# A written-out order of 840 tasks, laid anew: attention with a decaying state and a SiLU layer on one core

## The chip, the core and the metric

The kernel runs on one core of one Trainium2 chip. A core has five engines that run side by side, each through its own list of instructions in order: PE (TensorE, matmuls and transposes; PEld is its loading of weights), ACT (ScalarE), DVE (VectorE), POOL (GpSimd) and SP (SyncE, which here only starts transfers). They wait for one another through semaphores, and DMA engines move data between HBM and the core's memory. The metric is the time of one execution in microseconds on the device. The span is the time from the first to the last instruction in the profiled execution.

## The reference

A recurrent attention over 768 steps, for 4 batches and 8 heads of 48 features, gives `x` of 3072 x 384, and a layer of width 2048 follows:

```python
f = 1.0 / (1.0 + np.exp(-f_logit))
for t in range(S):                      # S = 768, B = 4, H = 8, D = 48
    state = f[:, :, t, :, None] * state + np.einsum('bhd,bhe->bhde', k[:, :, t], v[:, :, t])
    y[:, :, t] = np.einsum('bhd,bhde->bhe', q[:, :, t], state)
x = y.transpose(0, 2, 1, 3).reshape(B * S, H * D)
h = x @ w_in                            # 384 x 2048
g = h * (1.0 / (1.0 + np.exp(-h)))
out = g @ w_out                         # 2048 x 384
```

Inputs and outputs are of float32; the kernel's matmuls are of bf16.

## The kernel before

**Tiles.** The 768 steps are cut into 6 chunks of 128. A chunk of a batch is a unit, of which there are 24, and two units make a pair; `PAIRS` lists 12. Pairs 0 to 3 (kind `T`) hold the first two chunks of one batch. Pairs 4 to 11 (kind `N`) hold the same chunk of two batches. In a chunk the running product of `f` is a sum of logarithms, done by a matmul with a triangular matrix; the queries are divided and the keys multiplied by its exponential, so that the recurrence becomes a masked product of 128 x 128, and a state of 48 x 48 for each head passes from chunk to chunk.

**Tasks.** The work of a pair `P` and, where it has one, of a unit `i` is cut into tasks. A word such as `qkD.9.0:S:1` of the string `PLAN` names task, pair and unit, then the engine (P = PE, A = ACT, V = DVE, G = POOL, S = SP) and the numbers of the buffers that it takes anew. The tasks are:

- `f`, `q`, `k`, `v`: loads (L227), of a pair or, where a word has two of them, of half a pair. `E`, `L`: exp (L233) and ln (L237, L240) on ACT. `cs`: the cumulative sum on PE (L304 to L314). `a`, `ia`: its exponentials on ACT (L316). `al`: the decay over a chunk, on ACT (L255, L318).
- `qg`, `ki`: queries and keys times those (L321). `vb`: `v` as bf16. `tq` and `qkc`: in pairs 0 to 3, PE transposes of `qk` (L328) and their copy. `qkD`: in pairs 4 to 11, a DMA transpose of `qk` in their place (L336).
- `sc`: scores on PE (L345, L349). `at`: the mask, on DVE (L353). `y` and `yi`: the output of attention on PE (L262, L361, L365). `d`, `sd`, `su`: the new state, on PE (L274, L382), DVE or ACT (L386, L181) and POOL (L392, two instructions each).
- `yc`: `y` as bf16. `yT` and `xc`: PE transposes of it (L373) and their copy, for pairs 0 to 5 and 9 and unit 1 of pair 6; `yD`: a DMA transpose in their place (L377).
- `mi.P.j` (L248): two of the 16 column blocks of `x @ w_in` for both units, six matmuls of 128 x 256. `si.P.j` (L253): their SiLU on ACT. `mo.P.i.n` (L285): four of the 16 matmuls of `g @ w_out` for one unit. `oc` and `so`: the copy of the result and its store (L296, where pairs 0 to 3 take two DMAs, and L298).
- `wi`, `wo`: loads of the weights, issued by POOL. `idle.W.n`: n matmuls of W columns on zeros (L435), with no result.

**What sets the order.** Nothing is planned at run time or by the compiler: the last loop of the kernel goes through the words of `PLAN` and emits them, so each engine has its tasks in the order in which they stand there. The first four loads are emitted ahead of all else. An engine waits where a task needs what another has not done yet, or a buffer that is still read. The number of buffers of each class is in `SLOTS` (for instance six for `q`, four for `hT`, eight PSUM banks `pb`), and which of them a task takes stands in its word. SP issues loads, stores and DMA transposes in one list, so a wait there holds all that is behind it.

**ACT's tables.** Exp and ln need one table of functions on ACT, SiLU another. Where two tasks that follow each other on ACT in the plan need different ones, a load of the table (L484) is emitted ahead of the second:

```python
modes = [(n, mode_of(kind)) for n, (kind, *_) in enumerate(plan) if mode_of(kind)]
turns = {n2: TABLES[m2] for (_, m), (n2, m2) in zip(modes, modes[1:]) if m != m2}
```

Copies on ACT need neither, and stand where they stand.

Of the kernel before, what the change touches and what calls it, by code (L numbers as in the profile page):

```python
# [43 lines left out]
al.1:A:5 qg.0.0:G:2 ki.0.1:V:3 idle.512.1::2 idle.256.1::2 cs.2.1:P:0 ia.2.1:A:2 sd.1.0:A:1 qg.0.1:V: y.1:P:1,2 ki.0.0:G: tq.0.0:P:6 q.2.0:S:4
su.1.0:G:0 tq.0.1:P:7 wi.0:G: a.2.1:A:1 al.2:A:1 yc.1.0:V:2 cs.2.0:P:5 yT.1.0:P:1 qkc.0.1:V:1 qkc.0.0:A: yi.1.1:P: sc.0.0:P:0,7 xc.1.0:V:0 yc.1.1:A:0
al.0:A:2 vb.0.1:A:3 at.0.0.0:V:0 yT.1.1:P:6 sc.0.1:P:2,1 vb.0.0:G:4 at.0.0.1:V: d.0:P:0,4 wi.2:G: xc.1.1:A: sd.0.0:A:0 at.0.1.1:V:1 at.0.1.0:V:
ia.2.0:A:3 su.0.0:G:0 mi.1.2:P:6 wo.0:G: mi.1.3:P:0 wo.1:G: y.0:P:1,2 yi.0.1:P: a.2.0:A:4 sd.1.1:V:1 k.2.0:S:4 mi.1.6:P:3 yc.0.0:A:0 yT.0.0:P:5
# [12 lines left out]
L.4.0:A:1 mo.2.1.3:P: mo.2.0.1:P: at.3.1.1:V: oc.2.1:A:0 qkD.5.0:S:3 E.6.0:A:0 L.6.0:A:2 vb.5.0:A:5 at.3.0.1:V: qkD.5.1:S:2 sd.3.1:V:1 sc.5.0:P:3,0  # L60
at.5.0.1:V:0 at.5.0.0:V: y.3:P:2,4 v.5.1:S: vb.5.1:G:6 sc.5.1:P:5,6 at.5.1.1:V:1 yi.3.1:P: cs.4.1:P:7 a.4.1:A:0 so.0.1:S: k.4.1:S:5 at.5.1.0:V:
mo.2.0.2:P: k.6.0:S:2 q.6.0:S:0 yc.3.0:A:1 yc.3.1:A:0 al.4.1:A:5 mo.2.0.3:P: oc.2.0:A:4 ia.4.1:A:2 y.5.0:P:6 cs.6.0:P:3 a.6.0:A:3 yc.5.0:V:2 q.4.1:S:4
yT.3.0:P:4 yT.3.1:P:0 xc.3.1:V:1 su.3.1:G:0 xc.3.0:V: cs.6.1:P:1 q.4.0:S: f.7.0:S:2 ki.4.1:V:1 ia.6.1:A:4 y.5.1:P:2 yc.5.1:V:1 yT.5.0:P:0 cs.4.0:P:6
# [453 lines left out]
```

## Time and profile before

| what | value |
|---|---|
| median of 3 runs | 176.43 us (175.55 to 177.61) |
| the profiled execution | 176.43 us |
| its span | 174.7 us, 4734 instructions |
| mean granted clock of PE | 0.998 |
| PE busy | 168.0 us (96%) |
| ACT busy | 128.8 us (74%) |
| DVE busy | 77.9 us (45%) |
| POOL busy | 64.6 us (37%) |
| moved by DMA | 32.12 MB, mean 184 GB/s |

In rows of groups there stand the line, the engine, the operation, what it writes and reads, and the count; then the busy time, the mean of one in ns, and the idle time ahead of it with what ended most of it. In rows of a timeline there stand the start, the duration, the engine, the line and the operation; in brackets the idle time before and what ended it. In the chain of waits SPq is the time that SP's queue took to issue.

### The profile page before, as it was taken

What the parts mean: (1) busy time and instruction counts of PE and PEld (TensorE: products, weight loads), DVE (VectorE), ACT (ScalarE), POOL (GpSimd) and SP (SyncE); (2) the same over time, 40 slices, a digit from 0 to 9 for tenths busy, and PEclk for the clock granted to TensorE, in tenths of its full rate; (3) what the DMA queues carried; (4) which work ended last, traced back from release to release, by engine and by line L of the source; (5) the groups of instructions that cost most, each with busy time, mean ns of one, the idle gap of its engine ahead of it and who ended that gap; (6) DMA issues with size and microseconds to landing.
All of it is one profiled execution on the core that took longest, in us unless ns stands there. A gap on an engine that the chain in (4) does not pass through costs nothing.

```text
span 174.7 us, 4734 instructions
## 1 busy us (share of the span) xinstructions
PE 168.0 (96%) x1921; PEld 125.1 (72%) x1921; DVE 77.9 (45%) x163; ACT 128.8 (74%) x236; POOL 64.6 (37%) x110
## 2 busy tenths in 40 slices
PE   7989999999999999999999999999998999999992
PEld 2547888666876897866786696776785866877870
DVE  7388700527749933245672421435912674410010
ACT  3799697384999999968888899887778741273811
POOL 6087891032484350224627004940053376100000
PEclk9999999999999999999999999999999999999999
DMA  5999999989958989899998895998995999221321
GB/s 142 324 325 218 267 201 203 280 204 234 220 110 184 203 171 207 191 199 181 195 228 178 159 231 132 241 189 170 193 186 153 208 145 238 82 45 40 140 94 45
DMA packets 110677, 32.12 MB, mean 184 GB/s; under 512 B 104096, under 2 KB 110528, under 8 KB 110656
## 3 DMA queue, kind: packets, MB, share of 16 engines
...
q10 hardware_dynamic: 672, 0.33, 0.6%
...
q14 instruction: 6, 0.05, 0.1%
HBM read 25.17 MB, written 4.72 MB: 171 GB/s over the span
## 4 chain that ended last, share of the span: by engine, by line
PE 77%; DMA 10%; SPq 5%; POOL 3%; ACT 2%; issue 1%; POOLq 0%
PE pb L248 33%; PE pb L285 31%; SPq L227 4%; DMA f<-in_f_logit_dram 4%; DMA k<-in_k_dram 3%; PE pb L349 2%; PE pb L361 2%; DMA qkT<-qk 2%; POOL qk L321 2%; PE pb L365 2%; PE pb L373 1%; DMA xT<-yb 1%; PE pb L311 1%; PE pb L328 1%; PE pb L382 1%
## 5 line engine op out<-in xcount | busy, mean ns | idle before, releaser
L285 PE MATMUL pb<-w_out_sb,hT 128*128 128x384 bf16 (+2 forms) x400 | 70.2, 320 | 0.0
L248 PE MATMUL pb<-xT,w_in_sb 128*128 128x256 bf16 x576 | 68.7, 273 | 0.6 <-DMA xT<-yb 0.6
L253 ACT ACTIVATE hT<-pb 128x512 bf16<-128x512 f32 x96 | 51.2, 612 | 22.3 <-PE pb L248 21.7
L248 PEld LDWEIGHTS <-w_in_sb 128*128 128x128 bf16 x576 | 55.1, 98 | 9.4 <-issue 0.8
L285 PEld LDWEIGHTS <-hT 128*128 128x128 bf16 x400 | 36.4, 98 | 19.1
L392 POOL TENSOR_TENSOR st<-sd,al 48x192 bf16<-48x192 f32 x40 | 20.5, 512 | 23.1 <-PE pb L361 8.8
L316 ACT ACTIVATE x<-pb 128x384 f32<-128x384 f32 x48 | 21.2, 505 | 5.1 <-PE pb L308 2.5
L353 DVE TENSOR_TENSOR atm<-pb,triu 128x512 bf16<-128x512 f32 x32 | 20.0, 683 | 9.7 <-PE pb L349 9.5
L321 POOL TENSOR_TENSOR qk<-k,x 128x384 bf16<-128x384 f32 x15 | 15.4, 1037 | 21.9 <-DMA k<-in_k_dram 11.7
L484 ACT ACT_TABLE_LOAD x17 | 21.8, 1283 | 0.3
L183 DVE COPY ob<-pb 128x384 f32<-128x384 f32 (+1 forms) x14 | 7.5, 534 | 22.9 <-ACT hT L253 13.4
L183 POOL CAST vb<-v 128x384 bf16<-128x384 f32 x16 | 8.9, 560 | 20.4 <-DMA v<-in_v_dram 20.1
L321 POOL TENSOR_TENSOR qk<-q,x 128x384 bf16<-128x384 f32 x9 | 9.2, 1031 | 18.2 <-ACT hT L253 11.6
L386 DVE TENSOR_TENSOR sd<-pb,st 128x384 f32<-128x384 f32 x16 | 8.8, 552 | 15.3 <-PE pb L382 7.1
L321 DVE TENSOR_TENSOR qk<-q,x 128x384 bf16<-128x384 f32 x15 | 9.3, 622 | 9.1 <-ACT x L316 4.2
L233 ACT ACTIVATE e<-f 128x768 f32<-128x768 f32 x12 | 10.1, 843 | 3.8 <-DMA f<-in_f_logit_dram 3.7
L353 DVE TENSOR_TENSOR atm<-pb,mask 128x512 bf16<-128x512 f32 x16 | 10.0, 683 | 3.2 <-PE pb L345 2.9
L183 DVE CAST yb<-pb 128x384 bf16<-128x384 f32 x13 | 7.1, 553 | 9.1 <-PE pb L365 4.1
L183 DVE COPY qkTT<-pb 128x1024 bf16<-128x1024 bf16 x6 | 4.1, 690 | 11.0 <-PE pb L328 10.9
L181 ACT COPY ob<-pb 128x384 f32<-128x384 f32 (+1 forms) x11 | 5.1, 470 | 5.2 <-PE pb L285 5.1
L435 PE MATMUL pb<-zero 128*128 128x512 bf16 (+1 forms) x20 | 7.1, 507 | 1.2 <-DVE halves L467 1.2
L181 ACT CAST yb<-pb 128x384 bf16<-128x384 f32 x11 | 5.2, 481 | 3.1 <-PE pb L365 2.2
...
## 6 DMA issues: line engine op xcount, KB each, us to landing
...
```

Source lines behind the costliest of these rows:

```text
L181: nc.scalar.copy(dst, src)
L183: ENG[eng].tensor_copy(dst, src)
L233: return nc.scalar.activation(e, at("f", P)[:, j * w:(j + 1) * w], AF.Exp, scale=-1.0)
L248: nc.tensor.matmul(h[:, i, cols], w_in_sb[:, kk, n * 128:(n + 1) * 128], at("xT", P)[:, kk, cols], start=(kk == 0), stop=(kk == KT - 1))
L253: return nc.scalar.activation(at("hT", P)[:, 2 * j:2 * j + 2, :], at("h", P, j).rearrange("p (n c) -> p n c", n=2), AF.Silu)
L285: nc.tensor.matmul(at("o" + key, P, i)[:, 0:cols.stop - cols.start], at("hT", P)[:, n, i * C:(i + 1) * C], w_out_sb[:, n, cols], start=(n ...
L316: nc.scalar.activation(at(kind, P, i).rearrange("p h d -> p (h d)"), at("cs", P, i)[:, 0:HD], AF.Exp, scale=1.0 if kind == "ia" else -1.0)
L321: ENG[eng].tensor_mul(at("qk", P, i)[:, j, :, 0:D], heads("qk"[j], P, i), at("ia" if j else "a", P, i))
L353: ENG[eng].tensor_mul(at("atm", P, i)[:, r], at(f"s{r}", P, i).rearrange("p (n c) -> p n c", c=C), mask[:, None, :].to_broadcast([C, NP, C]))
L386: nc.vector.tensor_add(at("sd", P, i), d_ps, prev_state(P, i))
L392: nc.gpsimd.tensor_mul(at("st", P, i)[lo:lo + D, :, r * D:(r + 1) * D], at("sd", P, i)[lo:lo + D, :, r * D:(r + 1) * D], al_of(P, i)[lo:lo ...
L484: nc.scalar.preload_act_table_set(turns[n])
```

## The change

The string `PLAN` is written anew. Code, pairs, buffers and their numbers are as before. The set of tasks is the same too, but for the idle matmuls: 17 of 512 columns become 18, and 3 of 256 become 4, in other places. Some 60 tasks change their engine: eight `vb` go from POOL to ACT and five from DVE to POOL, seven `ki` from POOL to DVE, six `qg` from DVE to POOL, six `yc` from ACT to DVE and four back, five `oc` from ACT to DVE. Loads of ACT's table become 19, from 17. Of the rows of the string, one of each side stands here for all; a line of the new kernel has a number that is higher by one, since the string has a row more.

```diff
@@ -37,70 +37,71 @@
 PLAN = """
...
-mo.7.0.0:P:7 sc.9.1:P:6,1 sc.9.0:P:4,5 at.9.1.0:V:1 at.9.0.0:V:3 si.7.5:A: mi.7.6:P:3 si.7.7:A: si.7.3:A: mo.7.0.1:P: at.9.0.1:V: at.9.1.1:V:
...
+mo.7.0.0:P:3 yT.9.0:P:5 sc.8.0:P:2,4 xc.9.1:V:3 ia.10.1:A:2 sc.8.1:P:0,6 L.11.0:A:1 mo.7.1.2:P: xc.9.0:V: su.9.1:G:0 mi.9.1:P:5 mi.9.4:P:1 si.9.4:A:2
...
 """
```

ACT, where the last SiLUs of pair 7 and those of pair 9 are, before: `si.7.6`, `yc.9.0`, a table load, `ia.10.1`, `a.10.1`, `E.11.0`, `L.11.0`, a table load, `si.9.2`, `si.9.6`. (`hT` is written by a `si`, `x` by an `ia` or `a`, `e` by an `E`, `lf` by an `L`.)

```order
L253 ACTIVATE hT_123<-pb_143 128x512
L181 CAST yb_117<-pb_144 128x384
L484 ACT_TABLE_LOAD
L316 ACTIVATE x_91<-pb_145 128x384
L316 ACTIVATE x_90<-pb_145 128x384
L233 ACTIVATE e_83<-f_63 128x768
L240 ACTIVATE lf_86<-e_83 128x16x48
L484 ACT_TABLE_LOAD
L253 ACTIVATE hT_122<-pb_145 128x512
L253 ACTIVATE hT_122<-pb_143 128x512
```

The same place in the new plan: `si.7.7`, a table load, `a.10.1`, `E.11.0`, `ia.10.1`, `L.11.0`, a table load, `si.9.4`, a table load, `a.11.0`, a table load, `si.9.3`.

```order
L254 ACTIVATE hT_122<-pb_144 128x512
L485 ACT_TABLE_LOAD
L317 ACTIVATE x_92<-pb_141 128x384
L234 ACTIVATE e_84<-f_61 128x768
L317 ACTIVATE x_90<-pb_141 128x384
L241 ACTIVATE lf_86<-e_84 128x16x48
L485 ACT_TABLE_LOAD
L254 ACTIVATE hT_124<-pb_141 128x512
L485 ACT_TABLE_LOAD
L317 ACTIVATE x_91<-pb_140 128x384
L485 ACT_TABLE_LOAD
L254 ACTIVATE hT_124<-pb_141 128x512
```

The exponential `a.11.0`, which stood with `ia.11.1` in a later phase of its table, now stands alone between two SiLUs of pair 9, with a table load on either side. The cast `yc.9.0` is on DVE.

SP, where the DMA transposes of pair 9's `qk` are issued (`xT` is written by a `yD`, `qkT` by a `qkD`, `out_dram` by a store). Before: `so.5.1`, `yD.7.0`, `yD.7.1`, `v.9.0`, `so.5.0`, `so.4.0`, `qkD.9.0`, `qkD.9.1`.

```order
L298 DMA out_dram<-ob_135 128x384
L377 DMA_TRANSPOSE xT_118<-yb_115 128x3x128
L377 DMA_TRANSPOSE xT_118<-yb_116 128x3x128
L227 DMA v_78<-in_v_dram 128x16x48
L298 DMA out_dram<-ob_134 128x384
L298 DMA out_dram<-ob_139 128x384
L336 DMA_TRANSPOSE qkT_106<-qk_96 128x8x128
L336 DMA_TRANSPOSE qkT_108<-qk_93 128x8x128
```

After: `so.4.0`, `qkD.9.1`, `yD.7.0`, `yD.7.1`, `v.9.0`, `so.0.0` (two DMAs), `qkD.9.0`, `f.11.0`.

```order
L299 DMA out_dram<-ob_138 128x384
L337 DMA_TRANSPOSE qkT_105<-qk_94 128x8x128
L378 DMA_TRANSPOSE xT_120<-yb_115 128x3x128
L378 DMA_TRANSPOSE xT_120<-yb_116 128x3x128
L228 DMA v_81<-in_v_dram 128x16x48
L297 DMA out_dram<-ob_134 64x384 x2
L337 DMA_TRANSPOSE qkT_106<-qk_93 128x8x128
L228 DMA f_61<-in_f_logit_dram 128x16x48
```

The two transposes of pair 9 are apart: `qkD.9.1` has moved ahead of the two `yD.7`, and `so.0.0` stands directly in front of `qkD.9.0`.

SP, where pair 8's `yb` is transposed. Before: `so.1.0` (two DMAs), `q.11.0`, `q.10.0`, `k.10.0`, `k.11.0`, `so.6.0`, `yD.8.1`, `so.7.1`, `yD.8.0`.

```order
L296 DMA out_dram<-ob_136 64x384 x2
L227 DMA q_73<-in_q_dram 128x16x48
L227 DMA q_76<-in_q_dram 128x16x48
L227 DMA k_69<-in_k_dram 128x16x48
L227 DMA k_65<-in_k_dram 128x16x48
L298 DMA out_dram<-ob_134 128x384
L377 DMA_TRANSPOSE xT_119<-yb_117 128x3x128
L298 DMA out_dram<-ob_137 128x384
L377 DMA_TRANSPOSE xT_119<-yb_115 128x3x128
```

After: `qkD.8.1`, `q.11.0`, `q.10.0`, `k.11.0`, `k.10.0`, `so.6.0`, `yD.8.1`, `yD.8.0`, `so.4.1`, `so.5.1`.

```order
L337 DMA_TRANSPOSE qkT_107<-qk_97 128x8x128
L228 DMA q_71<-in_q_dram 128x16x48
L228 DMA q_74<-in_q_dram 128x16x48
L228 DMA k_65<-in_k_dram 128x16x48
L228 DMA k_69<-in_k_dram 128x16x48
L299 DMA out_dram<-ob_134 128x384
L378 DMA_TRANSPOSE xT_120<-yb_116 128x3x128
L378 DMA_TRANSPOSE xT_120<-yb_115 128x3x128
L299 DMA out_dram<-ob_135 128x384
L299 DMA out_dram<-ob_139 128x384
```

`so.1.0` and `so.7.1` are no longer here, and the two `yD` of pair 8 stand one behind the other.

Counted over the whole plan, a store stands directly in front of a DMA transpose on SP nine times before and nine times after, at other places.

More of the change, by code (lines that the diff above doesn't have):

```diff
@@ L44 @@
[L44 to L47, printed above, removed]
@@ L60 @@
[L60 to L63, printed above, removed]
@@ new lines @@
+v.1.0:S:2 a.1.0:A:0 cs.1.1:P:2 idle.256.1::3 a.1.1:A:3 qg.1.0:V: qg.1.1:V:3 idle.512.1::6 ia.1.1:A:1 vb.1.0:G:5 ki.1.1:V: idle.512.4::5 tq.1.0:P:7
+qkc.1.0:V:1 f.2.0:S:1 wi.1:G: idle.512.1::0 tq.1.1:P:5 idle.512.1::1 idle.512.1::7 qkc.1.1:V: E.0.0:A:0 L.0.0:A:2 wi.3:G: cs.0.0:P:7 ia.0.0:A:3
+k.0.0:S:2 E.2.0:A:1 q.0.0:S:4 a.0.0:A:4 sc.1.0:P:3,0 sc.1.1:P:5,4 L.2.0:A:1 cs.0.1:P:1 vb.1.1:G:3 al.0:A:5 at.1.0.1:V:2 ia.0.1:A:0 al.1:A:0
+at.1.0.0:V: ki.0.0:G:1 d.1:P:6,0 idle.256.1::3 at.1.1.0:V:0 at.1.1.1:V: a.0.1:A:3 qg.0.0:G: cs.2.1:P:3 al.2:A:2 y.1:P:2,7 idle.256.1::4 a.2.1:A:1
@@ new lines @@
+si.3.1:A: si.3.5:A: mi.3.4:P:3 ki.6.1:V:0 yc.5.0:V:2 si.3.4:A: v.4.0:S: mi.3.0:P:6 ki.4.1:G:4 yT.5.1:P:1 si.3.0:A: cs.4.0:P:2 yT.5.0:P:5 qg.6.1:V:
+xc.5.1:V:1 vb.4.1:V:2 mi.3.7:P:3 xc.5.0:V: d.5.1:P:6 mo.3.1.0:P:0 ia.6.0:A:2 al.6.0:A:0 v.6.0:S:0 qg.6.0:V:3 so.2.1:S: a.4.0:A:4 mi.5.0:P:7 qg.4.0:G:1
+ia.4.0:A:3 al.4.0:A:3 mi.3.6:P:5 mo.3.1.1:P: si.5.0:A:2 mi.5.3:P:1 si.5.3:A: mi.5.2:P:4 mo.3.0.0:P:2 mo.3.0.1:P: si.3.6:A: si.3.7:A: d.4.1:P:1
+mo.3.0.2:P: mo.3.0.3:P: qg.4.1:V: ki.4.0:V: sd.5.1:V:0 qkD.4.1:S:2 si.5.2:A: mi.5.4:P:7 si.5.4:A: oc.3.0:A:5 mi.5.5:P:5 mi.5.6:P:6 qkD.4.0:S:1
@@ new lines @@
+si.5.5:A: si.5.6:A: mi.5.1:P:2 vb.6.1:V:0 mi.5.7:P:4 sc.4.1:P:7,5 ki.6.0:V: qkD.6.1:S:0 sd.4.1:V:1 sc.4.0:P:3,6 qkD.6.0:S:3 su.5.1:G:0 si.5.1:A:
+at.4.0.1:V:0 at.4.1.1:V:1 at.4.1.0:V: mo.5.0.0:P:1 si.5.7:A: vb.4.0:A:5 mo.3.1.2:P: mo.3.1.3:P: d.4.0:P:2 vb.6.0:A:4 at.4.0.0:V: E.9.0:A:1 mo.5.0.1:P:
+y.4.0:P:5 sc.6.0:P:7,4 E.7.0:A:0 oc.3.1:V:1 sc.6.1:P:0,6 L.7.0:A:1 at.6.0.0:V:2 mo.5.1.0:P:3 q.7.0:S:2 mo.5.1.1:P: L.9.0:A:2 sd.4.0:V:0 y.4.1:P:7
+cs.7.1:P:2 yc.4.1:V:2 a.7.1:A:3 al.7.1:A:1 at.6.1.1:V:0 yc.4.0:A:0 mo.5.1.2:P: mo.5.1.3:P: d.6.0:P:5 cs.7.0:P:7 ia.7.1:A:4 at.6.0.1:V: yT.4.0:P:2
@@ new lines @@
+at.6.1.0:V: xc.4.0:A:3 su.4.1:G:0 yT.4.1:P:6 v.7.0:S:0 vb.7.1:G:1 su.4.0:G:0 al.7.0:A:4 xc.4.1:A: a.7.0:A:1 mo.5.0.2:P: mo.5.0.3:P: ia.7.0:A:0
+k.7.0:S:1 so.1.1:S: qg.7.1:G:4 mi.4.1:P:0 mi.4.0:P:6 so.3.1:S: sd.6.0:V:0 si.4.1:A:0 mi.4.4:P:4 d.6.1:P:2 y.6.0:P:7 v.8.0:S:3 mi.4.7:P:0 f.8.0:S:2
+oc.5.0:V:4 vb.7.0:V:6 qg.7.0:V:2 si.4.0:A: y.6.1:P:1 yc.6.1:A:0 mi.4.5:P:6 mi.4.2:P:5 si.4.7:A: yc.6.0:V:2 ki.7.1:V: si.4.2:A: so.5.0:S: mi.4.3:P:0
+k.9.0:S:3 mo.4.0.0:P:7 mi.4.6:P:5 si.4.4:A: si.4.3:A: si.4.5:A: so.3.0:S: si.4.6:A: vb.8.1:A:0 ki.7.0:V: su.6.0:G:0 qkD.7.1:S:2 mo.4.0.1:P:
@@ new lines @@
+su.7.0:G:0 mi.6.3:P:3 mi.6.7:P:1 si.6.6:A: si.6.2:A: si.6.4:A: yc.7.0:A:0 y.7.1:P:6 si.6.3:A: yc.7.1:V:1 si.6.7:A: yD.7.0:S:2 yD.7.1:S: d.7.1:P:5
+mo.6.0.0:P:4 cs.8.1:P:3 mo.6.1.0:P:2 mo.6.1.1:P: mo.6.0.1:P: E.10.0:A:1 ki.9.0:G: v.9.0:S:4 a.8.0:A:0 so.0.0:S: al.8.1:A:2 L.10.0:A:2 mo.6.1.2:P:
+qg.8.0:G:3 ia.8.0:A:2 ia.8.1:A:4 al.8.0:A:3 mo.6.1.3:P: cs.10.0:P:0 qkD.9.0:S:1 a.8.1:A:3 ia.10.0:A:0 a.10.0:A:1 oc.6.1:V:4 sd.7.1:V:0 ki.8.0:V:
+vb.8.0:V:6 qg.8.1:V:4 mo.6.0.2:P: mo.6.0.3:P: mi.7.1:P:6 oc.6.0:V:0 si.7.1:A:0 ki.8.1:G: su.7.1:G:0 mi.7.5:P:7 d.8.1:P:0 mi.7.3:P:5 mi.7.0:P:2
@@ new lines @@
+at.8.1.1:V:3 at.8.1.0:V: mo.7.0.1:P: at.8.0.0:V:2 so.6.0:S: y.8.1:P:2 at.8.0.1:V: mi.9.2:P:4 cs.11.0:P:0 a.11.0:A:3 yc.8.1:V:1 yD.8.1:S:2 y.8.0:P:1
+d.9.0:P:6 mo.7.0.2:P: su.8.1:G:0 ki.10.0:G:0 yc.8.0:V:0 mi.9.3:P:1 mi.9.0:P:2 sd.9.0:V:0 qg.10.0:V: ki.10.1:G:1 yD.8.0:S: mo.7.1.3:P: mo.7.0.3:P:
+so.4.1:S: si.9.3:A: si.9.1:A: si.9.0:A: mo.9.0.0:P:1 si.9.2:A: so.5.1:S: d.8.0:P:6 v.10.0:S:3 oc.7.0:A:0 cs.11.1:P:4 qg.10.1:G: mo.9.1.0:P:5
+qkD.10.0:S:3 a.11.1:A:0 sd.8.0:V:1 mi.9.7:P:6 mi.8.6:P:3 qkD.10.1:S:0 ia.11.1:A:1 ia.11.0:A:4 so.6.1:S: ki.11.0:V:3 su.8.0:G:0 si.8.6:A:3 mo.9.1.1:P:
@@ new lines @@
+mi.9.5:P:2 v.11.0:S:5 si.9.5:A: mi.9.6:P:0 ki.11.1:V:1 si.9.6:A: qg.11.0:G: si.9.7:A: mi.8.1:P:4 mo.9.1.2:P: su.9.0:G:0 mo.9.0.1:P: mo.9.1.3:P:
+mi.8.7:P:6 oc.7.1:A:5 mo.9.0.2:P: oc.9.1:V:1 vb.10.0:A:3 qg.11.1:G: mo.9.0.3:P: oc.9.0:V:4 si.8.1:A: vb.10.1:A:1 si.8.7:A: sc.10.1:P:5,3 so.9.1:G:
+at.10.1.0:V:0 sc.10.0:P:4,7 at.10.0.1:V:1 at.10.0.0:V: qkD.11.0:S:1 mi.8.3:P:2 mi.8.0:P:1 so.9.0:G: so.2.0:G: mi.8.4:P:6 at.10.1.1:V: si.8.0:A:
+si.8.4:A: mi.8.2:P:0 vb.11.0:A:0 y.10.0:P:5 si.8.3:A: y.10.1:P:6 yc.10.0:V:0 qkD.11.1:S:2 mo.8.0.0:P:1 mi.8.5:P:3 so.7.1:S: yc.10.1:A:2 sc.11.1:P:7,6
```

91 lines of the change are left out of this document (36 added, 55 removed).

## The prediction

> **What bounds the kernel now.** I read the busy time by stretches first, then PE's waits, then the chain of waits in order of time, then the timelines of the engines at the places the change touches. The first view gives, for each stretch, its start and end, its length and then each engine's busy time: PE, weight load, DVE, ACT, POOL, the granted clock, the DMA share and GB/s.
>
> ```profile
> 18.00:130.00 112.00, 111.78 (x1320) 85.58 (x1317) 53.35 (x101) 94.17 (x171) 43.65 (x64) 1.00 1.00 199
> 130.00:135.00 5.00, 4.39 (x33) 2.74 (x32) 1.02 (x2) 4.54 (x9) 1.96 (x3) 1.00 0.47 130
> 135.00:171.20 36.20, 36.18 (x351) 27.62 (x348) 11.09 (x19) 16.28 (x31) 8.85 (x15) 1.00 0.56 122
> PE pb L248 <- DMA xT<-yb: 0.6, 1, 0.6
> PE pb L349 <- DMA qkT<-qk: 0.2, 1, 0.2
> ```
>
> PE is solid. From 18.0 to 171.2 us it idles 0.22 + 0.61 + 0.02 us, and the last two rows (PE's waits: sum, count, longest) say for what: once a `mi` task (L248) waits 0.6 for a DMA transpose of `yb` (a `yD`), once a `sc` task (L349) 0.2 for a DMA transpose of `qk` (a `qkD`). The clock is 1.00 throughout. PE does the same matmuls in both plans, so no order can gain more than 0.83 there. What can move the time is the run-in up to 18.0, where PE waits for the other engines, and any new idle time of PE after it. The tail is the same: the last pieces on PE are still a `mo`, then one `oc` on ACT and one `so` on SP. The profiled execution took 176.43 us, which is also the median shown; its span is 174.7, and 1.73 lies around it.
>
> **The start.** Up to `mi.1.2`, the first `mi`, the set of PE tasks is the same. These rows are of the timeline.
>
> ```profile
> 7.18 1.13 PE L435 MATMUL pb<-zero 128*128 128x512 bf16 x5
> ...
> 9.39 0.62 PE L328 MATMUL pb<-ident,qk 128*128 128x128 bf16 x8 [0.33 <-DVE qk L321]
> ...
> 10.14 0.32 PE L304 MATMUL pb<-lf,tincl 128*128 128x384 bf16 x1
> ...
> 14.30 0.47 ACT L181 COPY sd<-pb 128x384 f32<-128x384 f32 x1
> ...
> 15.04 0.20 ACT L255 ACTIVATE al<-pb 128x8 f32<-128x8 f32 x1
> 15.10 1.05 ACT L181 COPY qkTT<-pb 128x1024 bf16<-128x1024 bf16 x1
> ...
> 17.99 1.48 PE L248 MATMUL pb<-xT,w_in_sb 128*128 128x256 bf16 x12
> ```
>
> The chain to `mi.1.2` runs through `cs.0.0` on PE (10.14), `sd.1.0` on ACT (14.30), `su` on POOL and `yi` on PE. The new plan has two more idle matmuls of 512 columns ahead of `cs.0.0`: 2 x 1.13/5 = 0.45, of which 0.13 falls into the gap between 10.01 and 10.14, so +0.3. Two `al` stand ahead of `sd.1.0` on ACT, where before there was none; from the start of one to the start of the next task took 0.06 (15.04 to 15.10), so +0.1. `vb.1.1` leaves ACT for POOL, but ACT was waiting where it stood, so this gives nothing. `q.0.0` now reuses the buffer that `qg.1.1` frees; behind the loads already issued that wait is covered. Sum +0.4; bounds: -0.2, where the idle matmuls only fill time in which PE waits and the earlier loads tell, to +0.9, both edits at their whole durations and `q.0.0` uncovered.
>
> **The load of pair 3 and `d.2`.** The row of L392 is a group of the page (busy, mean ns).
>
> ```profile
> 24.70 1.95 POOL L321 TENSOR_TENSOR qk<-k,x 128x384 bf16<-128x384 f32 x2
> 35.97 0.69 POOL L183 CAST vb<-v 128x384 bf16<-128x384 f32 x1 [9.32 <-DMA v<-in_v_dram]
> ...
> L392 POOL TENSOR_TENSOR st<-sd,al 48x192 bf16<-48x192 f32 x40 | 20.5, 512 | 23.1 <-PE pb L361 8.8
> 38.53 0.51 PE pb L262 x32
> ```
>
> `k.3.0` waits on SP for `ki.2.0` and `ki.2.1` on POOL (done at 26.65). Now POOL does `su.0.1` and `su.1.1` first, two instructions of 0.51 each, so 2.05, and with their waits up to 2.9. `k.3.0` goes out that much later, and `f.3.0` and `v.2.0` queue behind it; `v.2.0` also stands behind `f.3.0` now. `v.2.0` landed at about 35.97, and `y.2` and `d.2` need its cast, at 38.5: 2.5 us of cover, of which the cast takes 0.69. The landing there is set by the queue of the weight loads, not by the issue, so most of 2 to 3 us of delay is absorbed: I take +0.2, between 0 and +1.9 (2.5, the middle of the delay, and 1.2 for `f.3.0`, half of an issue row of two loads below, less the 1.8 of cover that is left).
>
> **The ACT tables.** `a.11.0` now stands alone between two SiLUs (`si.9.4` and `si.9.3`), and `a.11.1` makes a phase of its own: 19 table switches instead of 17. Rows of the chain and of the timelines at this place before:
>
> ```profile
> 28.95 1.30 PE pb L285 x8
> 30.70 0.65 PE pb L248 x6
> 118.67 0.16 PE pb L311
> 121.22 0.40 PE pb L373 x6
> 122.27 0.55 PE pb L349 x16
> 143.39 0.17 PE pb L361 x4
> 143.56 0.20 PE pb L365 x8
> ...
> 116.55 0.83 PE L248 MATMUL pb<-xT,w_in_sb 128*128 128x256 bf16 x6
> ...
> 117.41 0.60 ACT L253 ACTIVATE hT<-pb 128x512 bf16<-128x512 f32 x1 [0.50 <-PE pb L248]
> 119.74 1.28 ACT L484 ACT_TABLE_LOAD   x1
> 121.03 0.87 ACT L316 ACTIVATE x<-pb 128x384 f32<-128x384 f32 x2
> 122.67 0.84 ACT L240 ACTIVATE lf<-e 128x768 bf16<-128x768 f32 x1
> 124.82 0.60 ACT L253 ACTIVATE hT<-pb 128x512 bf16<-128x512 f32 x1
> ...
> 129.69 2.07 ACT L253 ACTIVATE hT<-pb 128x512 bf16<-128x512 f32 x4 [0.83 <-PE pb L248]
> ```
>
> A switch costs 1.31: `L.11.0` ends at 123.51, the next SiLU starts at 124.82. SiLUs in a row start 0.5 apart (the last row: four end 2.07 after the first starts). Take the start of `mi.7.7` on PE as zero. Its SiLU starts at 0.86 (116.55 to 117.41) and ends at 1.46. Then, in the new order on ACT: switch, `a.10.1` from 2.77 (0.43 with its neighbour), `E.11.0` and `L.11.0` (0.84 each) with `ia.10.1` between, to 5.08; switch, `si.9.4` 6.39 to 6.99; switch, `a.11.0` 8.30 to 8.79; switch, `si.9.3` 10.10, `si.9.1` 10.60, `si.9.0` 11.08 to 11.68. `mo.9.0.0` reads their results: it can start at 11.73. PE's pieces from `mi.7.7` up to it are six `mi` of 0.65 (3.90), seven `mo` of 0.65 (4.55), four `y` of 0.37 (1.48), two `cs` of 0.16, two `yT` of 0.20, one `d` (four matmuls as in L361, 0.17) and the pair of `sc`, 0.55: 11.37. So PE waits 0.36. On the same clock `si.9.2` and `oc.7.0` end at 12.54; switch, `a.11.1` and the two `ia` to 15.1; switch, `si.8.6` 16.41, `si.9.5` to 17.5. PE reaches `mo.9.1.2`, which needs it, after eight `mi` and `mo` (5.20), a `d` and a `cs` (0.33), at 17.26, and could start at 17.55 by the same 0.05 from end to start: 0.29. Together +0.65, which the rows' rounding makes +0.6; bounds 0 (ACT reaches this place 0.6 ahead of PE) and +1.3 (one switch not covered). In a sentence of its own: the Trainium skill, "ScalarE: Activation LUTs", section "What ACT_TABLE_LOAD costs", gives 1283 ns for the load and about 1380 ns for a drain in front of it; the load agrees with the 1.28 here, but the 1.31 from end of work to next start leaves no room for the drain. By the page, an estimate, these six switches would cost 8.1 more and the sum would be 184.9.
>
> **The store moves and SP's queue.** There are nine stores directly in front of a DMA transpose in the old plan and nine in the new one, so the words of the change hold for some places and not as a count. What counts is what stands ahead of each transpose. SP's timeline and, at the end, the chain (SPq is SP's queue):
>
> ```profile
> 43.99 2.46 SPq L227 DMA_DIRECT2D f<-in_f_logit_dram  x2
> 50.15 2.69 SPq L336 DMA_TRANSPOSE qkT<-qk  x2
> ...
> 110.80 2.69 SPq L336 DMA_TRANSPOSE qkT<-qk  x2
> 113.53 1.23 SPq L296 DMA_DIRECT2D out_dram<-ob  x2
> ...
> 147.13 0.57 SPq L298 DMA_DIRECT2D out_dram<-ob  x1
> DMA to landing us min/median/max: 3.1/3.3/6.1
> 115.99 0.62 PE L349 MATMUL pb<-qkT 48*128 48x128 bf16 x16
> 130.45 1.18 SPq L377
> 131.69 0.56 SPq L298
> 132.34 2.28 DMA xT<-yb
> ```
>
> SP issues back to back from 50.15 to 147.70: 1.35 for a `qkD`, 1.2 for a `yD`, about 0.6 for a store and 1.23 for a store in two halves. So a transpose goes out when the queue reaches it, and each thing put ahead delays it. The only wait is 46.45 to 50.15, 3.70 us, for the `ki` in front of `qkD.5.0`. The new plan puts `v.5.1` and the halves of `so.0.1` into that wait, ahead of `qkD.5.0`; they were behind it. That makes a lead of 1.0 + 1.3 = 2.3 for all later entries, less what the wait no longer holds; I take 2.1 (1.45 to 2.75).
>
> - `yD.8.0`, the 0.61 stall: it landed at 134.62. The pair `so.1.0` (1.23), `so.5.1` and `so.7.1` (0.6 each) no longer stand ahead: 2.4 earlier without the lead, about 130 with it. PE needs it for `mi.8.6` at 131.3 to 131.8, so the stall goes: -0.61.
> - `qkD.7.0`, the 0.22 stall: one store less ahead (0.66) and the lead: -0.22.
> - `qkD.9.0`: it landed at 110.80 + 3.3 = 114.1. Added ahead are `qkD.9.1` (1.35) and the halves of `so.0.0` (1.23 and a gap of 0.05), gone is `so.5.1` (0.6): +2.05 without the lead, 114.05 with it. `sc.9.0` was at 115.99; it comes earlier by `mi.7.4`, `mi.7.7` and `mo.7.0.0` (0.65 each), later by `d.8.1` (0.17), 1.78 earlier, and with the gone stall and the start's 0.6 stands at 114.6. No stall by 0.5 us; 0.6 of lead less, and there is one.
>
> The other transposes that come later (`yD.6.0` and `yD.7.1` by 2.0, `yD.11.0` by 0.6) have 0.5 to 2 us left with the lead.
>
> Sum: 176.43 + 0.4 + 0.2 + 0.6 - 0.83 = **176.8**.
>
> **The rivals.**
>
> *Faster.* All new waits are covered: the two idle matmuls fill time PE would wait anyway, ACT reaches the switches with 0.6 in hand, `v.2.0` is early enough. Then only the two stalls and 0.2 of the start go: 176.43 - 0.83 - 0.2 = 175.4. For it: ACT is busy 94.17 of 112.00, so it has slack before that place. Against it: the chain on ACT is counted from a SiLU that PE itself releases.
>
> *Slower.* SP gains no lead: `ki.5.0` on its engine comes as late as the queue did, or `so.0.1` and `v.5.1` themselves wait longer than the 3.70. Then `qkD.9.0` lands at 116.1 and `sc.9.0` waits 1.5 on PE for it: 176.8 + 1.5 = 178.3, and up to 3 more with a landing of 6.1 instead of 3.3. It decides once the lead is below 1.5. For it: the margin of 0.5 rests on an average queue. Against it: `ki.5.x` is the only wait seen.
>
> *The stores' order does nothing.* The place of a store ahead of a transpose changes no landing, and the 0.61 stall stays: 176.8 + 0.6 = 177.4. Against it speaks the chain, in which a store of 0.56 stands between the two `yD`. In a sentence of its own: the Trainium skill, "DMA: Bandwidth & Descriptors", section "Issuing engines are not separate DMA queues", holds that initiating a transfer on the sequencer is usually small beside the transfer; this trace disagrees, with 1.35 of SP's time for a transpose that lands in 3.3.
>
> *A drain at each switch.* Each of the six switches waits for ACT's work as long again as the load takes, because two SiLUs around a single `a.11.0` cannot run on: 6 x 1.28 = 7.7, 184.5. Against it: 1.31 at both switches of this stretch.
>
> **How the numbers follow.** Runs of one kernel here spread from 175.55 to 177.61, so about 1% (174.67 to 178.19) is what a measurement can tell from no change. Forecast 0.45, with its own range 175.9 to 178.0 from the bounds of the start, `d.2` and the tables; faster rival 0.22, slower 0.21, stores do nothing 0.10, drain 0.02. Faster by over 1%: 0.10 of the 0.22, since 175.4 lies 0.7 above the bound, and 0.02 of the forecast: 0.12. Slower: 0.18 of the slower rival, 0.07 of the forecast with `d.2` and the tables at their upper ends, 0.02 of the stores, 0.02 of the drain: 0.29. The same: 0.59. The range goes from the faster rival less 0.4 (the start's cover gained as well) to the slower rival with 0.6 of further lateness: 175.0 to 178.9; outside stay the drain, the far end of the slower rival and some of the faster one.
>
> **What would show it.** In the new profile PE's wait at L248 for `xT` should be gone and idle time of about 0.4 and 0.3 stand at L285 for `hT`, right behind the lone table pair; the first `mi` should start at 18.4; SP's wait near 46 should be 1.5 to 2 us; `sc.9.0` should not wait for `qkT`. I am wrong if PE waits at L349 for more than 1 us, if L274 of the old numbering waits for a late `v.2.0`, or if PE's idle time after 18 is below 0.2.

## The result, and the profile after

The new order is slower: 178.68 us (median of 22 runs, 177.13 to 179.56) against 176.45 (22 runs, 175.55 to 181.38). The ratio is 1.0108, with a 95% interval of 1.0077 to 1.0139. That lies inside the range of the prediction (175.0 to 178.9) and just past its bound for "slower"; its likeliest number was 176.8, no change. Here and below, medians are of all runs, while ratios leave out the runs in a slower state, which both kernels have. The 22 runs lie in two groups, ten from 177.1 to 178.3 and twelve from 178.7 to 179.6; the profiled one is of the lower group. The profiled execution of the new order took 177.42 us, with a span of 175.6, so 0.99 above the profiled one of before.

PE's waits in the changed kernel (engine, line, what it waited for: us in total, times, the longest), and its rows in two views of the timeline at the two places:

```profile
PE pb L350 <- DMA qkT<-qk: 1.5, 2, 1.0
PE pb L436 <- DVE halves L468: 1.2, 1, 1.2
PE pb L305 <- ACT lf L238: 1.0, 2, 0.6
```

```profile
17.88 1.48 PE L249 MATMUL pb<-xT,w_in_sb 128*128 128x256 bf16 x12
...
98.18 0.40 PE L350 MATMUL pb<-qkT 48*128 48x128 bf16 x8 [0.58 <-DMA qkT<-qk]
...
115.77 0.62 PE L350 MATMUL pb<-qkT 48*128 48x128 bf16 x16 [0.95 <-DMA qkT<-qk]
```

The wait of `mi` for `xT` (0.61 before) is gone. In its place `sc.7.0` waits 0.58 us for `qkD.7.0` and `sc.9.0` waits 0.95 for `qkD.9.0`. The first `mi` starts 0.11 earlier (17.99 before). Busy time by stretches, in the columns of the prediction's first view:

```profile
18.00:90.00 72.00, 71.91 (x895) 55.64 (x894) 38.05 (x71) 61.91 (x114) 28.96 (x43) 1.00 1.02 204
90.00:110.00 20.00, 19.42 (x195) 14.45 (x193) 5.66 (x12) 18.52 (x36) 6.37 (x8) 1.00 0.92 190
110.00:130.00 20.00, 19.05 (x219) 14.70 (x217) 13.27 (x24) 17.39 (x28) 4.82 (x8) 1.00 0.99 185
130.00:171.70 41.70, 41.61 (x391) 31.50 (x391) 11.55 (x20) 22.54 (x43) 9.64 (x13) 1.00 0.50 119
```

PE idles 0.58 in the stretch of `sc.7.0`, 0.95 in that of `sc.9.0`, 0.18 elsewhere. ACT has left a trace in rows that count as busy. The twelve matmuls of `mo.7.1.3`, `mo.7.0.3` and `mo.9.0.0` take 2.21 us to the next start, and twelve of 0.1625 (a `mo` of four took 0.65) are 1.95:

```profile
128.67 2.38 PE L286 MATMUL pb<-w_out_sb,hT 128*128 128x384 bf16 x12
130.88 0.33 PE L383 MATMUL pb<-vb,qk 128*128 128x96 bf16 x4
...
135.79 2.23 PE L286 MATMUL pb<-w_out_sb,hT 128*128 128x384 bf16 x12
137.85 0.38 PE L249 MATMUL pb<-xT,w_in_sb 128*128 128x256 bf16 x2
```

So 0.26 goes there, in small pieces between matmuls, and 2.06 less 1.95, so 0.11, at the second place, which holds `mo.9.1.2`. The account of the two profiles is then: start -0.11, waits of before -0.83, `sc.7.0` +0.58, `sc.9.0` +0.95, behind the table loads +0.37. The sum is +0.96, against 0.99 measured (the 0.18 is partly in the 0.37 and is not counted again).

### The profile page after: what moved, and what is told of

It reads as the page before. It is cut to its first block, busy times and chain, and to the rows that moved or that the text cites. A ratio compares the mean times of both kernels' runs of the same rounds, so it can differ in the third digit from the quotient of the medians.

```text
span 175.6 us, 4737 instructions
## 1 busy us (share of the span) xinstructions
PE 167.8 (96%) x1924; PEld 125.5 (71%) x1924; DVE 81.5 (46%) x167; ACT 133.8 (76%) x243; POOL 60.3 (34%) x101
## 4 chain that ended last, share of the span: by engine, by line
PE 72%; ACT 8%; DMA 8%; issue 4%; DVE 4%; SPq 2%; POOL 1%; DVEq 0%
PE pb L286 29%; PE pb L249 28%; DMA qkT<-qk 6%; PE pb L350 2%; PE pb L329 2%; DMA f<-in_f_logit_dram 2%; ACT x L317 2%; ACT hT L254 2%; PE pb L362 2%; ACT L485 1%; DVE atm L354 1%; PE pb L366 1%; PE pb L346 1%; PE pb L436 1%; SPq L297 1%
## 5 line engine op out<-in xcount | busy, mean ns | idle before, releaser
L286 PE MATMUL pb<-w_out_sb,hT 128*128 128x384 bf16 (+2 forms) x400 | 70.6, 320 | 0.1
L286 PEld LDWEIGHTS <-hT 128*128 128x128 bf16 x400 | 36.6, 98 | 20.0 <-ACT hT L254 0.8
L317 ACT ACTIVATE x<-pb 128x384 f32<-128x384 f32 x48 | 21.8, 503 | 3.2 <-PE pb L305 1.2
L184 DVE COPY ob<-pb 128x384 f32<-128x384 f32 (+1 forms) x16 | 8.6, 538 | 25.8 <-PE pb L286 24.6
L322 POOL TENSOR_TENSOR qk<-k,x 128x384 bf16<-128x384 f32 x11 | 11.6, 1061 | 15.9 <-ACT x L317 7.8
L322 POOL TENSOR_TENSOR qk<-q,x 128x384 bf16<-128x384 f32 x12 | 12.9, 1078 | 9.9 <-DMA q<-in_q_dram 4.0
L322 DVE TENSOR_TENSOR qk<-k,x 128x384 bf16<-128x384 f32 x13 | 9.8, 762 | 9.7 <-ACT x L317 6.3
L184 DVE CAST yb<-pb 128x384 bf16<-128x384 f32 x15 | 8.1, 554 | 7.2 <-PE pb L366 6.4
L184 POOL CAST vb<-v 128x384 bf16<-128x384 f32 x8 | 4.4, 546 | 14.8 <-DMA v<-in_v_dram 14.8
L184 DVE COPY xT<-pb 128x384 bf16<-128x384 bf16 x10 | 3.6, 356 | 10.5 <-PE pb L374 10.5
L322 DVE TENSOR_TENSOR qk<-q,x 128x384 bf16<-128x384 f32 x12 | 6.8, 577 | 2.8 <-DMA q<-in_q_dram 2.8
L182 ACT COPY ob<-pb 128x384 f32<-128x384 f32 (+1 forms) x9 | 4.2, 468 | 4.7 <-PE pb L286 4.6
```

The source lines that it names most:

```text
L184: ENG[eng].tensor_copy(dst, src)
L286: nc.tensor.matmul(at("o" + key, P, i)[:, 0:cols.stop - cols.start], at("hT", P)[:, n, i * C:(i + 1) * C], w_out_sb[:, n, cols], start=(n ...
L317: nc.scalar.activation(at(kind, P, i).rearrange("p h d -> p (h d)"), at("cs", P, i)[:, 0:HD], AF.Exp, scale=1.0 if kind == "ia" else -1.0)
L322: ENG[eng].tensor_mul(at("qk", P, i)[:, j, :, 0:D], heads("qk"[j], P, i), at("ia" if j else "a", P, i))
```

## The experiments

Unless a sentence says otherwise, each starts from the changed kernel and alters what is named, nothing else. Time is the median; the ratio is to the kernel before on the same chip. "PE idle" is the sum of the gaps of PE between the start of `mi.1.2` and the last matmul in the profiled execution, worked out from the records of the matmuls; the same sum gives 0.84 for before and 1.72 for the changed kernel. r1 to r4 ran on one chip, r5 to r8 on a second, r9 to r12 on a third.

| run | runs | us | ratio (95%) | PE idle | waits for a transpose: `sc.7.0`, `sc.9.0` |
|---|---|---|---|---|---|
| r1 changed again | 12 | 176.90 | 1.0049 (1.0016 to 1.0081) | 1.43 | 0.11, 0.86 |
| r9 changed, a third time | 12 | 177.23 | 1.0057 (1.0023 to 1.0091) | 1.14 | none, 1.04 |
| r2 so.0.0 behind qkD.9.0 | 6 | 179.35 | 1.0111 (1.0031 to 1.0191) | 1.86 | 0.20, other cause |
| r3 wait of SP unfilled | 12 | 177.21 | 1.0058 (1.0015 to 1.0100) | 1.63 | 0.54, 1.06 |
| r5 so.0.0 on POOL | 12 | 176.83 | 1.0009 (0.9959 to 1.0059) | 0.33 | none |
| r8 so.0.0, so.3.0 on POOL | 12 | 176.38 | 1.0014 (0.9975 to 1.0054) | 0.09 | none |
| r10 the same, chip of r9 | 12 | 176.01 | 1.0001 (0.9965 to 1.0038) | 0.23 | none |
| r6 lone table pair gone | 10 | 177.78 | 1.0103 (1.0060 to 1.0145) | 2.10 | 0.17, 1.14 |
| r7 qkD.8.0 ahead | 4 | 180.78 | 1.0243 (1.0169 to 1.0317) | 4.92 | 0.68, other cause |
| r12 two idle matmuls out | 1 | 177.81 | - | 2.25 | 0.98, 1.19 |
| r4 before, two stores moved | 12 | 175.89 | 1.0009 (0.9969 to 1.0049) | 0.00 | none |
| r11 before, three stores moved | 12 | 176.63 | 1.0035 (1.0008 to 1.0061) | 0.30 | 0.28, none |

In r4 the median is below that of before (176.16) and the ratio, which is not the quotient of the two medians, above 1: the two are the same within what this can tell. One run of r10, at 436 us, lies far off all others; the median isn't moved by it.

**The changed kernel again (r1, r9).**

> The changed kernel once more, for a second profiled execution beside the first. The 22 runs of it lie in two groups, 177.1 to 178.3 and 178.6 to 179.6, and the profiled one (177.42) is of the lower group. Theory Q (the transposes of pairs 7 and 9 go out late on SP's queue): the same two waits of L350 for qkT, 0.6 and 1.0 us or, in an execution of the upper group, about 1.3 us more in total at the same two places. Rival E (the loss lies elsewhere and the first profile does not show it): waits at another line, or PE's matmuls themselves longer.

> The changed kernel a third time, on one chip with the next run, since the two ratios so far (1.011 and 1.005) are of different chips. Theory Q: sc.9.0 waits 0.9 to 1.1 us for qkD.9.0 again, and the median is 0.8 to 1.5 us above that of the next run.

Rows of PE's timeline with a wait, r1 and then r9:

```profile
56.51 0.40 PE L350 MATMUL pb<-qkT 48*128 48x128 bf16 x8 [0.46 <-DMA qkT<-qk]
115.55 0.62 PE L350 MATMUL pb<-qkT 48*128 48x128 bf16 x16 [0.86 <-DMA qkT<-qk]
```

```profile
114.93 0.62 PE L350 MATMUL pb<-qkT 48*128 48x128 bf16 x16 [1.04 <-DMA qkT<-qk]
```

The wait at `sc.9.0` is in every profile of this order, 0.86 to 1.04 us. The other one comes and goes: at `sc.7.0` in the first profile, at `sc.5.1` in r1 (0.46, with 0.11 at `sc.7.0`), nowhere in r9. The ratios, 1.005 and 1.006, are lower than in the first 22 runs. No profile of the unaltered order is of an execution above 178.6, so what these 22 runs lost beyond the 1.0 us of the profile isn't seen. The profiled executions of r6 and r12 (177.81 both) have more idle time, 2.10 and 2.25 us: in r12 both waits are longer, in r6 that at `sc.9.0` is, and `sc.5.1` waits too (0.41).

**Does filling SP's wait give a lead (r3)?** The edit moves two words of the plan behind `qkD.5.1`:

```diff
-... v.5.1:S: ... so.0.1:S: ... qkD.5.0:S:1 ... qkD.5.1:S:0
+... qkD.5.0:S:1 ... qkD.5.1:S:0 v.5.1:S: so.0.1:S:
```

> The changed kernel with v.5.1 and so.0.1 behind qkD.5.1, as before the change, instead of in front of qkD.5.0. The prediction's step: SP issues them inside a wait, which gives everything behind them 2.1 us; without them there qkD.9.0 would go out about 2.1 us later and sc.9.0 wait about 3 us, so about 2 us slower than the changed kernel. Rival B (SP is held by transfers that are still on their way, so that what is put into the wait costs as much time elsewhere): qkD.5.0 goes out 2 to 3 us earlier, qkD.9.0 at the same time within 0.7 us, and the time is the changed kernel's within 0.5 us.

SP's timeline, the changed kernel and then r3:

```profile
44.18 3.60 SPq L228 DMA_DIRECT2D f<-in_f_logit_dram  x2
47.88 3.04 SPq L297 DMA_DIRECT2D out_dram<-ob  x2
51.03 2.71 SPq L337 DMA_TRANSPOSE qkT<-qk  x2
53.79 0.58 SPq L228 DMA_DIRECT2D v<-in_v_dram  x1
...
110.34 2.01 SPq L297 DMA_DIRECT2D out_dram<-ob  x2
112.45 1.27 SPq L337 DMA_TRANSPOSE qkT<-qk  x1
```

```profile
42.67 3.27 SPq L228 DMA_DIRECT2D f<-in_f_logit_dram  x2
48.28 3.60 SPq L337 DMA_TRANSPOSE qkT<-qk  x2
51.93 0.57 SPq L228 DMA_DIRECT2D v<-in_v_dram  x1
52.56 1.27 SPq L297 DMA_DIRECT2D out_dram<-ob  x2
53.87 0.61 SPq L228 DMA_DIRECT2D v<-in_v_dram  x1
...
112.23 1.27 SPq L337 DMA_TRANSPOSE qkT<-qk  x1
```

The numbers are those of rival B; its cause, transfers still on their way, isn't shown. With the wait unfilled `qkD.5.0` goes out 2.75 us earlier, since two things fewer stand ahead of it. The first entry behind all that was moved is `v.4.1`: it goes out at 53.79 with the wait filled and at 53.87 without. So filling the wait gave the queue a lead of 0.08 us, not of 2.1, and `qkD.9.0`, 60 us later, goes out at 112.45 with it and at 112.23 without. Two things are to be seen in the rows. The halves of `so.0.1` take 3.04 us of the queue in front of the transposes and 1.27 behind them: an issue row of this view can hold more than the instruction's own cost. What held the queue there the profile doesn't say. And in r3 the wait runs from 45.94 to 48.28, 2.3 us, while it was 3.7 in the order before: the last task that `qkD.5.0` reads from ends on POOL at 48.25, against 50.12, so there was less to fill.

**The store in front of qkD.9.0 (r2, then r5, r8 and r10).** First it was put behind:

```diff
-... so.0.0:S: al.8.1:A:2 ... cs.10.0:P:0 qkD.9.0:S:1
+... al.8.1:A:2 ... cs.10.0:P:0 qkD.9.0:S:1 so.0.0:S:
```

> The changed kernel with the store so.0.0 (two DMAs, 2.0 us on SP in the changed kernel's trace) behind qkD.9.0 instead of in front of it, nothing else moved. Theory Q: qkD.9.0 goes out 2.0 us earlier, the wait of 0.95 us in front of sc.9.0 goes, and the time falls by about 0.9 us (0.5%) against the changed kernel. Rival E: the wait goes, and the time stays within 0.3 us, since something else is late next. Rival S (the queue's place does not matter): qkD.9.0 lands when it did, and the wait stays.

`qkD.9.0` went out at 109.93 and landed at 113.7, in time. The time did not fall all the same: the profiled execution took 179.17 us, against 177.08 in r1, and the ratio, with an interval that overlaps that of r1, is no lower. PE's waits, a row of DVE's timeline and three stretches of r2:

```profile
PE pb L350 <- DVE ob L184: 1.3, 1, 1.3
114.91 0.56 DVE L184 COPY ob<-pb 128x384 f32<-128x384 f32 x1 [2.58 <-DMA out_dram<-ob]
114.00:116.00 2.00, 0.42 (x5) 0.20 (x4) 1.02 (x2) 0.18 (x1) 0.00 (x0) 1.00 0.97 197
116.00:118.00 2.00, 2.00 (x27) 1.67 (x27) 1.63 (x3) 0.60 (x1) 0.00 (x0) 0.89 1.79 230
118.00:121.00 3.00, 3.00 (x17) 1.90 (x16) 1.41 (x3) 1.48 (x3) 0.00 (x0) 0.50 0.76 146
```

The copy is `oc.6.0`. It takes the buffer that `so.0.0` empties, so it waits for the landing of that store, and `sc.9.0` takes the PSUM bank that `oc.6.0` reads. Moved back, the store held `sc.9.0` by this way instead. In the changed kernel this second way was nearly as late as the first (`oc.6.0` ended at 114.65, `sd.8.1` behind it, which frees the other bank, at 115.12, and the transpose landed at 115.73). Rival E was right in kind, since something else is late next, but not in size; rival S was wrong: the queue's place matters, and two things wait for the store.

So the store has to leave SP and still go out early. POOL is free there:

```diff
-so.0.0:S:
+so.0.0:G:
```

> The changed kernel with so.0.0 issued by POOL instead of SP, at its place in the plan. In the run with so.0.0 behind qkD.9.0, sc.9.0 waited for a copy on DVE instead: oc.6.0 takes the buffer that so.0.0 empties, and sc.9.0 the bank that oc.6.0 reads. So two things hold sc.9.0 in the changed kernel: qkD.9.0, which stands 2.0 us of stores further back, and oc.6.0, which waits for the landing of so.0.0. With so.0.0 off SP both come earlier. Theory Q: no wait of more than 0.1 us at sc.9.0, time 0.9 us below the changed kernel (ratio to before about 1.000). Rival E: the wait goes, and PE then waits about 0.4 us at mo.9.0.0 and 0.3 at mo.9.1.2 for SiLUs behind the extra table loads (L286, hT), which the wait at sc.9.0 had covered, so that 0.2 us are left of the gain.

and, for r8 and r10, `so.3.0:G:` too, which stands in front of `qkD.7.1` and `qkD.7.0`:

> The changed kernel with so.0.0 and so.3.0 issued by POOL. so.3.0 stands in front of qkD.7.1 and qkD.7.0; in two profiles of the changed kernel's order sc.7.0 waited 0.6 us for qkD.7.0 or was just in time. Theory Q: none of the waits for qkT is left, PE is busy from the first mi to the end, and the time is 1.4 us below the changed kernel, 0.7 below before (ratio 0.995). Rival E: waits of 0.3 to 0.7 us come up at mo.9.0.0 and mo.9.1.2, and the ratio is 0.998 to 1.000.

> The changed kernel with so.0.0 and so.3.0 issued by POOL, again, for a comparison with the changed kernel on one chip. Theory Q: no wait of PE for qkT, and a median 0.8 to 1.5 us below the changed kernel's. Rival E (the loss is not at these two places): less than 0.4 us below.

PE at this place in r5, and its stretches in r10:

```profile
112.11 2.13 PE L249 MATMUL pb<-xT,w_in_sb 128*128 128x256 bf16 x18
114.17 0.62 PE L350 MATMUL pb<-qkT 48*128 48x128 bf16 x16
```

```profile
18.00:110.00 92.00, 92.00 (x1094) 70.60 (x1092) 45.44 (x84) 81.21 (x152) 37.98 (x56) 1.00 1.03 203
110.00:120.00 10.00, 9.86 (x119) 7.82 (x119) 7.23 (x13) 8.31 (x14) 2.89 (x6) 1.00 1.09 182
120.00:170.00 50.00, 49.91 (x486) 37.77 (x486) 16.43 (x29) 30.62 (x53) 10.65 (x15) 1.00 0.61 133
```

No wait for `qkT` is left. `qkD.9.0` goes out at 110.08 in r5, 2.37 us earlier than in the changed kernel, and `oc.6.0` finds its buffer free. PE idles 0.33, 0.09 and 0.23 us in the three, of which 0.20 in r5 and 0.14 in r10 are in front of `mi.7.1`. On one chip the changed kernel took 177.23 and the version with two stores on POOL 176.01: 1.22 us less, ratios 1.0057 and 1.0001. On another chip r5 and r8 (1.0009, 1.0014) stand beside r6 (1.0103), which keeps the store where the change put it. This shows that the stores account for the loss as far as the later runs show one. r5 has it all with `so.0.0` alone; what `so.3.0` adds doesn't show. Moving them doesn't make a version better than before: r8 was expected at 0.995, and though its profile has no wait left, its ratio is 1.0014.

**The table loads (r6).**

```diff
-... mi.9.2:P:4 cs.11.0:P:0 a.11.0:A:3 ... qkD.10.0:S:3 a.11.1:A:0
+... mi.9.2:P:4 cs.11.0:P:0 ... qkD.10.0:S:3 a.11.0:A:3 a.11.1:A:0
```

> The changed kernel with a.11.0 next to a.11.1, so that the lone pair of table loads goes (17 instead of 19), nothing else moved. By the prediction's term this gives 0.6 us; by the changed kernel's trace, where mo.9.0.0 starts 0.05 us after si.9.0 and PE idles 0.1 there, it gives 0.1 to 0.2 us: the four SiLUs of pair 9 start 2.5 us earlier, PE no earlier. A drain at each switch, as long as the load, would make it 2.6 us earlier still.

```profile
128.88 2.11 PE L286 MATMUL pb<-w_out_sb,hT 128*128 128x384 bf16 x12
130.82 0.33 PE L383 MATMUL pb<-vb,qk 128*128 128x96 bf16 x4
...
136.60 1.80 PE L286 MATMUL pb<-w_out_sb,hT 128*128 128x384 bf16 x10 [0.38 <-ACT hT L254]
```

The 0.26 at `mo.9.0.0` is gone (128.88 to 130.82 is 1.94), but the phase of `a.11.1` is longer by `a.11.0`, and PE waits 0.38 behind it at `mo.9.1.2`, where it lost 0.11. Two loads less gain nothing that shows; the changed kernel itself did not run on this chip.

**The two idle matmuls (r12).** The edit takes `idle.512.1::1 idle.512.1::7` out.

> The changed kernel without the two idle matmuls of 512 columns in front of cs.0.0. By the prediction's term they cost 0.3 us of the start. By the changed kernel's trace, where mi.1.2 starts at 17.88 and ia.0.0 on ACT, which reads cs.0.0, at 10.39 after L.0.0 (done 9.75), cs.0.0 would start 0.4 earlier and mi.1.2 0 to 0.3 earlier. The wait of sc.9.0 stays.

```profile
17.87 1.38 PE L249 MATMUL pb<-xT,w_in_sb 128*128 128x256 bf16 x11
```

The first `mi` starts at 17.87, against 17.85 to 17.89 with them (the changed kernel, r1, r9). They cost nothing: without them PE waits 0.35 us for `L.0.0` in their place.

**Before without its own waits (r4, r11).** From the kernel before:

```diff
-so.6.0:S: ... yD.8.1:S:1 ... so.7.1:S: ... yD.8.0:S:
+... yD.8.1:S:1 ... yD.8.0:S: so.6.0:S: so.7.1:S:
```

> The kernel before with the stores so.6.0 and so.7.1 behind yD.8.0, and yD.8.1 and yD.8.0 side by side; nothing else moved. Theory Q: yD.8.0 goes out about 1.2 us or more earlier, the wait of 0.61 us of mi.8.2 goes, and the time is 0.4 to 0.6 us below before (ratio 0.997). Rival S (the stores' order does nothing): the wait stays and the ratio is 1.000.

and in r11 `so.3.0:G:` besides.

> The kernel before with so.6.0 and so.7.1 behind yD.8.0 and so.3.0 issued by POOL, so that both of its waits for a transpose go (0.61 at mi.8.2, 0.22 at sc.7.0). The best of what the runs point to. Theory Q: no wait of PE after 18 us and 0.5 to 0.9 us below before (ratio 0.995 to 0.997). Rival: the waits of before are there in some executions only, its fastest have none (175.2 to 175.6), and the median falls by less than 0.4 us.

In r4's profile `yD.8.0` goes out at 129.73 (132.34 before), the 0.61 is gone, PE has no gap at all after 18 us, and the span is 173.5. The place of a store does set when a transpose goes out. But the median falls by 0.27 us and the ratio is 1.0009, which can't be told from none, and r11 even stands 0.35% above before, though its profile shows 0.30 us of idle time against 0.84. Taking the wait of one profile away doesn't move the median. The rival's account, that the wait is in some executions only (the fastest of before, 175.1 to 175.6, have room for none), fits both but is argued: before has one profile. Why r11 is slower than before isn't settled; its profiled execution has a span 0.4 shorter than that of before.

**Later still (r7).** `qkD.8.0` was put in front of `qkD.9.0`. In the plan it then stands ahead of the `ki.8.0` that writes its keys, so that this kernel's keys of that one unit are those of an earlier one; the work of the engines is the same.

> The changed kernel with qkD.8.0 in front of qkD.9.0, which makes the wait at sc.9.0 longer by one transpose, 1.3 us, to 2.2 us. In the run with so.0.0 behind, PE idled 0.8 and 0.8 us between 114 and 116 us, and from 117 to 121 us the granted clock was 0.50. Theory C (a wait of PE of 1.5 us or more lowers the clock, shorter ones do not): the clock is near 0.5 for 3 to 4 us after the wait, and the time is up by 1.3 for the wait and 1.5 to 2 for the clock, about 3 us above the changed kernel. Rival W (the clock has nothing to do with the wait): 1.3 us above, clock 1.00.

```profile
117.06 0.56 DVE L322 TENSOR_TENSOR qk<-k,x 128x384 bf16<-128x384 f32 x1 [4.80 <-ACT hT L254]
118.87 0.21 PE L350 MATMUL pb<-qkT 48*128 48x128 bf16 x1 [2.76 <-DVE ob L184]
```

The edit did something else than was meant. `ki.8.0` on DVE (the first row) came only when the transpose had read the buffer (it landed at 116.98), `oc.6.0` stood behind it, and `sc.9.0` waited 2.76 us for the bank. The granted clock stayed at 1.00 through this wait, so theory C isn't borne out by this profile; the mean clock of the other executions says more (last section).

## Why the prediction was right and wrong, point by point

- **The bound and the floor.** Right. PE's work is the same; what moves the time is its idle time. Both waits of before were read correctly, and the one at `yD.8.0` went, as forecast: it lands at 131.18, 1.3 us before it is needed.
- **SP's lead of 2.1 us.** Wrong, and this is the step that failed. It rested on the reading that SP issues back to back from 50.15 to 147.70, each kind of instruction at its own cost, with one wait of 3.70. Rows of the kernel before that the prediction did not show, beside the 2.69 of two `qkD` and the 0.56 of a store that it did, tell otherwise:

```profile
115.50 4.43 SPq L336 DMA_TRANSPOSE qkT<-qk  x2
...
127.25 3.10 SPq L298 DMA_DIRECT2D out_dram<-ob  x1
...
131.69 0.56 SPq L298 DMA_DIRECT2D out_dram<-ob  x1
```

  In that stretch the stores and transposes alone take 17 us more than if each were as short as the shortest of its kind. So the rows ahead of an entry, added up, don't tell when it goes out. r3 measures what filling the wait gave: 0.08 us for the entry right behind, nothing for `qkD.9.0`. What holds the queue in these rows stays open. (The view of SP's own waits is no safe guide to it: it gives two waits of 1.9 us in all to L377, whose rows are as short as any, 1.18 to 1.22.)
- **`qkD.9.0`.** Right without the lead. The working had +2.05 for the queue and a need at 114.6. It went out 1.65 later than before, landed at 115.73, and PE could have started at 114.82. The wait is 0.95, where the slower rival had 1.5. This rival, with 0.21, is what happened at this place; r5, r8 and r10 show it. Of its two reasons, r3 bears out that `so.0.1` itself holds the queue, though for 3.04 and not for more than the 3.70.
- **`qkD.7.0`.** Forecast: the 0.22 goes. The plan does not have one store less ahead of it, as the working says, but one more (`so.5.0`), and `yD.6.0` has moved behind it. It lands 0.85 earlier than before (98.13 against 98.98), but PE gets to `sc.7.0` 1.2 us earlier (97.60 against 98.80), a move of the need that the working left out. 0.58 in the profile, 0.11 in r1, none in r9, 0.98 in r12.
- **What the working did not see at all**: `sc.9.0` also hangs on `oc.6.0` through a PSUM bank, and that on the landing of `so.0.0` through an output buffer (r2).
- **The start, +0.4.** Wrong by 0.5: -0.11. The plan has three more idle matmuls of 512 columns ahead of `cs.0.0`, 19 against 16, and not two; in all it has 19 against 17, where the text of the change says 18. They were added to PE's work, but the wait of `tq.1.1` for DVE that the prediction quoted (0.33) is gone in the new order, and `cs.0.0` can't start much earlier anyway, since it reads `L.0.0`. With two of them taken out (r12), it starts at 9.78 instead of 9.87, and the first `mi` no earlier. `sd.1.0` on ACT even starts earlier (13.92 against 14.30), with three `al` ahead of it instead of one: the exponentials ahead of it begin earlier, at 10.39 against 10.66.
- **`d.2`, +0.2.** 0: no wait there. `vb.2.0` is done at 37.48, 0.8 us later than before, and the first of `d.2` and `y.2` starts at 38.31.
- **The tables, +0.6.** The clock of ACT was right to a few hundredths at the first place, where `mo.9.0.0` starts 11.75 after `mi.7.7`, forecast 11.73, and 0.2 short at the second (`si.8.6` at 16.61, forecast 16.41). The wait was mis-sized, since PE's pieces took longer than the sum of their rows, and since half of `mo.9.1.2` reads `si.9.4`, which is done: 0.26 + 0.11 in place of 0.36 + 0.29. On the drain that a page of the Trainium skill gives, "ScalarE: Activation LUTs", section "What ACT_TABLE_LOAD costs", the changed kernel's trace decides as that of before did: from the end of `a.11.0` to the next SiLU it has 1.31 us with 1.28 of load.
- **The signs.** The wait for `xT` is gone, as said. The other signs of being right failed: the first `mi` starts at 17.88 and not at 18.4, near 46 SP shows no wait but a store of 3.04, `sc.9.0` waits for `qkT`, and the 0.26 and 0.11 at L286 show as busy. Of the three signs of being wrong one came true: PE's waits at the line of `sc` come to 1.5 us in all, over the 1 us named.
- **The number.** With the lead left out, the working's own terms give 176.8 + 1.5 = 178.3. That it lies near the first median is luck: the wait of `sc.9.0`, the start, `d.2` and the tables are all less than their terms, `sc.7.0` is more than its own, and the profiled execution shows 177.4, the later medians 176.9 and 177.2. The rest of the first median, 178.68, some 1.3 us, stands in no profile and stays open.
